# Reordering transposes and casts in a fused attention and feed-forward kernel

## The chip, the cores and the metric

The kernel runs on one core of one Trainium2 chip. The metric is the device time of one execution in microseconds (us), as the median of several runs. A profile of one execution gives the span of the core's instructions and the start and length of nearly all of them. Engines are called PE (TensorE), DVE (VectorE), ACT (ScalarE), POOL (GpSimd) and SP (SyncE, which only issues transfers here).

## The reference

Attention with 4 batches, 8 heads, 768 tokens and 64 columns a head. A query sees a key only if both fall to the same one of 16 centroids. Its output is the input of a gated feed-forward layer with 512 inputs and 1536 inner columns.

```
q_assign = argmax(q_n @ c_n.T); k_assign = argmax(k_n @ c_n.T)      # per head
scores   = where(q_assign == k_assign, q @ k.T / 8, -1e9)
x        = softmax(scores) @ v                                      # heads side by side: (3072, 512)
xn       = x / sqrt(mean(x*x) + 1e-6) * rms_g
out      = (silu(xn @ w_gate) * (xn @ w_val)) @ w_out
```

## The kernel before, in words

Work is cut into 8 units of 384 query tokens; a batch is two units. Heads are prepared in 8 groups of four, two groups to a batch. The order of everything is written out by hand: each engine runs its instructions in the order in which the Python code issues them, and waits on semaphores.

**Preparation of a head.** `trans(g, h, part)` turns q (part 0) or k (part 1) with three fp32 PE transposes into a PSUM tile `tq` (L208), which ACT or DVE copies to `qkT` (L214, L212). `cast` then copies `qkT` as bf16 into `qext` and `kext`, in two halves e = 0 and 1 (L227): q by POOL, k by DVE in the later groups. `vcast` casts v on POOL (L230). For a group, `cluster_products` (tile `sc`, L241) and DVE steps find each token's centroid as a one-hot row `oh`; `place` (L282) sends these rows by 8 small transfers for q and 8 for k into rows 64 to 79 of `qext` and `kext`, so that one product of 80 rows holds score and mask. Groups 0 and 1 use DVE transposes out of tables `pads` instead, whose unused columns POOL clears (L290, L571).

**Attention.** `scores(u, h, i)` makes two products into the PSUM tile `s` (two buffers, L332), and ACT takes the exponential into `pT` (L336); three such steps make a head of a unit. `pv` multiplies `pT` with v (`acc`, 18 products, L350), one head late: it is issued after the next head's second scores. The loop over a unit's 24 score steps is `attention`, which puts the other work between the steps: fixed hooks, or a list `fill` spread by its costs.

**Feed-forward.** In unit u the list holds the feed-forward of unit u - 1 and the output product of unit u - 2. `gv` makes `gate` and `val` (4 products of 384 columns each, L421). ACT takes the tanh of `gate` into `th` (L429), DVE multiplies it with `gate` again (L430), and a second DVE operation multiplies with `val` into `gvT` (L434). `out_mm` makes the output rows (`o`, L446).

**The shared PSUM buffers.** `tq`, `sc`, `gate`, `val`, `o` and the transposes of `xn` (`tx`) all take the next of three buffers of the pool `ps_g`, in the order of issue. So each of them waits until the one three places before it has been read for the last time: a `tq` by its copy, a `gate` by DVE's L430 (after ACT's L429), a `val` by DVE's L434.

**Where groups are prepared.** `group_work(g)` gives three lists: `t`, the 8 transposes in the order q, k of head 0, q, k of head 1 and so on; `c`, the casts (for each head one entry with POOL's q casts, `vcast`, the next loads and DVE's k cast of half 0, and one entry with DVE's k cast of half 1); and `a`, the centroid steps. `group(g)` orders them as two transposes and two cast entries of a head, then the next head. Groups 4 to 7 are spread with 16 of the `gate`/`val` entries in units 2 to 5. Group 3 is prepared in unit 1, in the list `prep`, after POOL's casts of group 2 (`norm`, which begins with a small POOL copy that waits for unit 0's normalised rows `xn`) and group 2's `vcast`, loads and centroid steps. `place` of group 2 is issued on SP, that of the others on POOL.

**Transfers.** SP's transfers cycle through eight semaphores in the built program, so each waits, besides its own data, for the landing of the transfer eight places before it. The weights are loaded from POOL's queue (`load_gv`, L194, and `load_o`, L197).

Of the kernel before, what the change touches and what calls it, by code (L numbers as in the profile page):

```python
# [22 lines left out]
def kernel(  # L23
# [12 lines left out]
    nc = tc.nc  # L36
    B, H, S, D = q.shape
    NC = centroids.shape[1]
# [6 lines left out]
    HG = 4  # L45
    NG = B * H // HG
    UNITS = [(b, c, HT) for b in range(B) for c in (0, HT)]
# [143 lines left out]
    def load_gv(i):  # L191
        c = slice(i * DF // 4, (i + 1) * DF // 4)
        for w, of in ((wg, moe_w_gate), (wv, moe_w_val)):
            nc.gpsimd.dma_start(out=w[:, :, c], in_=of[:, c].rearrange("(c p) f -> p c f", p=P))  # L194
# [34 lines left out]
    def vcast(n):  # L229
        nc.gpsimd.tensor_copy(vbf[n // HG % 4][:, n % HG, :, :D], stagedv[n])  # L230
# [46 lines left out]
    def place(on, g, m):  # L277

        ext = (kext if m else qext)[g % 4]
        for h in range(HG):  # L280
# [6 lines left out]

    pads = [(xp if p == 0 else outp).tile([P, NB, 32, 2], BF16, tag="o_sb" if p else "gvT", name=f"pads{p}")
            for p in range(H // 2)]
    nc.gpsimd.memset(pads[0][:, :, NC:], 0.0)  # L290

    def slot(n, m):

# [28 lines left out]
    def scores(u, h, i):  # L322
        b, col, nt = UNITS[u]
        g, hh, w = b * 2 + h // HG, h % HG, nt * P
        if i == 0:
            pT[u, h] = ptp.tile([P, ST, UQ], BF16, tag="pT", name="pT")
        n = ST // nt
        ps = ps_s.tile([P, 2, 512], F32, tag="s", name="s")
        flat = ps.rearrange("p a b -> p (a b)")
        for j in range(n):  # L330
            kc = n * i + j
            nc.tensor.matmul(ps[:, j, :w] if nt == HT else flat[:, j * w:(j + 1) * w],  # L332
                             lhsT=cols(kext[g % 4][:KR, hh], g, kc // HT, kc % HT * P, (kc % HT + 1) * P),
                             rhs=cols(qext[g % 4][:KR, hh], g, col // HT, 0, w), start=True, stop=True)
        of = ps[:, :, :w] if nt == HT else flat[:, :n * w].rearrange("p (c w) -> p c w", w=w)
        nc.scalar.activation(pT[u, h][:, n * i:n * i + n, :w], of, ACT.Exp, bias=off, scale=scale * ZS)  # L336
# [3 lines left out]
    def pv(u, h):  # L340
        b, _, nt = UNITS[u]
        g, hh = b * 2 + h // HG, h % HG
        if h == 0:
            xs[u] = xp.tile([P, HT, DM], F32, tag="x", name="x", bufs=2)
        if h % 2 == 0:
            accs[u] = ps_a.tile([P, 2, HT, D + 1], F32, tag="acc", name="acc")
        acc = accs[u]
        for t in range(nt):
            for kc in range(ST):
                nc.tensor.matmul(acc[:, h % 2, t], lhsT=pT[u, h][:, kc, t * P:(t + 1) * P],  # L350
                                 rhs=vbf[g % 4][:, hh, kc % HT * 2 + kc // HT], start=kc == 0, stop=kc == ST - 1)
        if h % 2:
            inv = small.tile([P, 2, HT], F32, tag="inv", name="inv")
            invs[u] = inv
            nc.vector.reciprocal(inv[:, :, :nt], acc[:, :, :nt, D])
            dst = xs[u][:, :nt, (h - 1) * D:(h + 1) * D].rearrange("p t (h d) -> p h t d", d=D)
            nc.vector.tensor_tensor(dst, acc[:, :, :nt, :D],  # L357
                                    inv[:, :, :nt].unsqueeze(3).broadcast_to([P, 2, nt, D]), op=ALU.mult)
# [6 lines left out]
    def squares(u, t, last):  # L365
        if (t, last) == (0, False):
            sq[u] = small.tile([P, 2, HT], F32, tag="ss", name="ss")
            xn[u] = xp.tile([P, HT, DM], BF16, tag="xn", name="xn")
        c = slice(DM - 2 * D, DM) if last else slice(0, DM - 2 * D)
        to = sq[u][:, int(last), t:t + 1]  # L370
        if u <= 1:
            nc.vector.scalar_tensor_tensor(xn[u][:, t, c], xs[u][:, t, c], 1.0 / DM, xs[u][:, t, c], op0=ALU.mult,
                                           op1=ALU.mult, accum_out=to)
        else:
            nc.scalar.activation(xn[u][:, t, c], xs[u][:, t, c], ACT.Square, scale=DM ** -0.5, accum_out=to)
# [90 lines left out]
    def group_work(g):  # L466

        t, c = [], []
        for h in range(HG):
            n = g * HG + h  # L470
            t += [(0.3, lambda h=h: trans(g, h, 0)), (0.3, lambda h=h: trans(g, h, 1))]

            def others(n=n):
                vcast(n)
                load_qk(n + NQ)
                load_v(n + NV)

            def both(h=h, f=others):
                cast(nc.gpsimd, g, h, 0)
                f()  # L480
                cast(nc.vector, g, h, 1, (0,))
            if g == 2:
                c.append((0.0, others))
            else:
                c += [(0.0, both), (0.0, lambda h=h: cast(nc.vector, g, h, 1, (1,)))]
        a = []
        for m in range(2):
            a += [(0.0 if i else 0.7, f) for i, f in enumerate(cluster_steps(g, m))]
            if g <= 3:
                a.append((0.0, lambda m=m: place(nc.sync if g == 2 else nc.gpsimd, g, m)))  # L490
        if g > 3:
            a.append((0.0, lambda: [place(nc.gpsimd, g, m) for m in range(2)]))
        return t, c, a

    def group(g):
        t, c, a = group_work(g)
        return [x for h in range(HG) for x in t[2 * h:2 * h + 2] + c[2 * h:2 * h + 2]] + a

    def spread(a, b):

# [10 lines left out]
    def ffn_work(u):  # L511
        n = UNITS[u][2] / HT
        w = [(0.18 * n, lambda c=c: xtrans(u, c)) for c in range(CC)]
        for f in range(FC):
            for val in (False, True):
                w.append((0.64 * n, lambda f=f, val=val: gv(u, f, val)))
        return w

    def out_work(u):
        return [(0.86, lambda t=t, p=p: out_mm(u, t, p)) for t in range(UNITS[u][2]) for p in range(3)]  # L520

    def border(o, ffn):

        return o[:-2] + ffn[:2] + o[-2:-1] + ffn[2:4] + o[-1:]
# [42 lines left out]
    casts(pool_, 0, Q1)  # L567
    casts(pool_, 1, Q1)
    vcast(0)
    for p in range(1, H // 2):  # L570
        nc.gpsimd.memset(pads[p][:, :, NC:], 0.0)  # L571
    load_gv(0)
    vcast(1)

# [53 lines left out]
    def attention(heads, fill, skip=0, hooks={}):  # L628
        gaps = [(u, h, i) for u, h in heads for i in range(UNITS[u][2])]
        total, done, n = sum(c for c, _ in fill), 0.0, 0  # L630
        for at, (u, h, i) in enumerate(gaps):
            scores(u, h, i)
            if i == min(1, UNITS[u][2] - 1):
                for p in due:
                    pv(*p)
                due[:] = [(u, h)]
            if h == H - 1:
                squares(u, i, False)
            if (u, h, i) in hooks:
                hooks[u, h, i]()  # L640
            while n < len(fill) and at >= skip and done <= total * (at + 1 - skip) / (len(gaps) - skip):
                done += fill[n][0]
                fill[n][1]()
                n += 1
        for _, f in fill[n:]:
            f()

    attention([(0, h) for h in range(H)], [], hooks={(0, *divmod(i, HT)): f for i in range(H * HT) for f in [first.get(i, more)] if f})
    for u in range(1, NU):
        ffn, o, g = ffn_work(u - 1), out_work(u - 2) if u > 1 else [], u + 2  # L650
        if u == 1:
            t, c, a = group_work(2)
            t3, c3, a3 = group_work(3)
            n = LEAD - 4
            prep = c + a + [x for h in range(HG) for x in t3[max(2 * h, n):2 * h + 2] + c3[2 * h:2 * h + 2]] + a3[:5]
            idle = const.tile([P, 1], BF16)

            def norm():
                rms(0)
                nc.gpsimd.tensor_copy(idle, xn[0][:, HT - 1, DM - 1:])  # L660
                for h in range(HG):
                    casts(pool_, H + h, K0, Q0, K1, Q1)
                    if h:
                        load_o((h - 1) * FC // 3)

            hooks = {(1, 0, 0): late[6], (1, 0, 1): lambda: (late[7](), norm())}
            hooks.update({(1, *divmod(2 + i, HT)): t3[i][1] for i in range(n)})
            hooks[1, *divmod(LEAD - 1, HT)] = lambda: (busy(4, False), xtrans_all(0))
            fill = spread(ffn[CC:CUT], prep)
            attention([(1, h) for h in range(H)], fill, LEAD, hooks)  # L670
        else:
            fill = ffn_work(u - 2)[CUT:] + [(0.0, lambda u=u: rms(u - 1))]
            fill += border(spread(o[:3], a3[5:]) + o[3:], ffn) if u == 2 else border(o, ffn)
            attention([(u, h) for h in range(H)], fill + spread(ffn[CC:CUT], group(g) if g < NG else []), 1)
# [41 lines left out]
```

The softmax here doesn't subtract the row's maximum and nothing guards it: scores larger than these inputs give would overflow.

## Time and profile before

| what | value |
|---|---|
| median of 8 runs | 349.37 us (348.44 to 349.99) |
| the profiled execution: time, span | 349.42 us, 347.6 us |
| PE busy | 338.5 us (97%) |
| ACT, DVE, POOL busy | 260.0 us (75%), 221.6 us (64%), 111.8 us (32%) |
| chain of work that ended last | PE 83%, ACT 6%, POOL 6%, DVE 3% of the span |

Busy time is that of the engine's instructions. An entry such as "PE ... [0.84 <-DVE th L430]" in the timeline says that PE sat idle for 0.84 us before this instruction, and that the DVE instruction on line 430 ended the wait. Each timeline row is start, length, engine, line, operation, output<-inputs, shape and how many were merged. A row for several matmuls begins with the first and ends with the last one's modelled end, which overlaps the next row's start.

### The profile page before, as it was taken

To read this page: it belongs to the slowest core of one execution; us is meant where nothing else is said; L and a number is where in the kernel's file an instruction comes from. 1 tells how busy PE (TensorE), PEld (TensorE's weight loads), DVE (VectorE), ACT (ScalarE), POOL (GpSimd) and SP (SyncE) were. 2 spreads that over 40 slices of the span, in tenths; PEclk is the share of its full clock that TensorE was granted. 3 is DMA by queue.
4 is the path that set the end of the run, shared out by engine and by line. 5 is a ranking of instruction groups with operands and counts; after the bars stand their busy time and mean duration, and the time that the engine had idled before them with its cause. 6 is when DMAs were issued, how large, how long until landed. Compare 5 with 4: busy or idle time off the path is not lost.

```text
span 347.6 us, 7983 instructions
## 1 busy us (share of the span) xinstructions
PE 338.5 (97%) x3039; PEld 208.0 (60%) x3039; DVE 221.6 (64%) x539; ACT 260.0 (75%) x449; POOL 111.8 (32%) x225
## 2 busy tenths in 40 slices
PE   8999999999999999999999999999999999999996
PEld 4547656555665557655675657755566656655553
DVE  6999686966568645786267854687456644675430
ACT  5899978766888769887787877978778877764321
POOL 5999595234344403371041801436000000000000
PEclk9999999999999999999999999999999999999999
DMA  7999999073350015401130001000100001001002
GB/s 277 395 180 256 251 176 284 28 235 123 107 183 29 16 60 159 147 17 40 60 93 2 23 33 62 0 6 19 62 32 0 2 33 60 2 1 63 30 2 91
DMA packets 27158, 31.62 MB, mean 91 GB/s; under 512 B 4464, under 2 KB 24176, under 8 KB 27120
## 3 DMA queue, kind: packets, MB, share of 16 engines
q1 hardware_dynamic: 18464, 25.02, 21.1%
q0 software_dynamic: 8368, 5.71, 10.2%
q8 instruction: 24, 0.39, 0.4%
q10 hardware_dynamic: 288, 0.39, 0.3%
q14 instruction: 14, 0.11, 0.1%
HBM read 28.35 MB, written 6.29 MB: 100 GB/s over the span
## 4 chain that ended last, share of the span: by engine, by line
PE 83%; ACT 6%; POOL 6%; DVE 3%; issue 1%; POOLq 0%; ACTq 0%; DVEq 0%
PE o L446 17%; PE val L421 17%; PE gate L421 17%; PE s L332 15%; PE acc L350 8%; ACT pT L336 4%; PE tq L208 3%; PE sc L241 3%; POOL kext L227 2%; POOL qext L227 2%; PE tx L395 1%; PE warm L117 1%; PE o L457 1%; DVE th L430 1%; POOL vbf L230 1%
## 5 line engine op out<-in xcount | busy, mean ns | idle before, releaser
L336 ACT ACTIVATE pT<-s,off 128x768 bf16<-128x768 f32 x192 | 170.8, 905 | 36.0 <-PE s L332 35.2
L332 PE MATMUL s<-qext,kext 80*128 80x384 bf16 x384 | 94.4, 327 | 2.6 <-ACT pT L336 0.8
L421 PE MATMUL gate<-xnT,wg 128*128 128x384 bf16 x384 | 78.4, 325 | 0.6 <-DVE gvT L434 0.4
L421 PE MATMUL val<-xnT,wv 128*128 128x384 bf16 x384 | 78.1, 326 | 0.8 <-DVE th L430 0.8
L430 DVE SCALAR_TENSOR_TENSOR th<-th,gate 128x384 f32<-128x384 f32 x84 | 46.4, 552 | 50.6 <-ACT th L429 50.5
L446 PE MATMUL o<-wo,gvT 128*128 128x512 bf16 x276 | 67.4, 379 | 0.0
L227 POOL CAST qext<-qkT 64x384 bf16<-64x384 f32 x64 | 34.4, 543 | 78.2 <-ACT qkT L214 54.4
L332 PEld LDWEIGHTS <-kext 80*128 80x128 bf16 x384 | 36.4, 98 | 33.3 <-issue 8.7
L421 PEld LDWEIGHTS <-wv 128*128 128x128 bf16 x384 | 36.1, 97 | 26.3 <-issue 4.6
L429 ACT ACTIVATE th<-gate 128x384 f32<-128x384 f32 x84 | 41.1, 490 | 14.3 <-PE gate L421 13.9
L434 DVE SCALAR_TENSOR_TENSOR gvT<-th,val 128x384 bf16<-128x384 f32 x84 | 46.2, 550 | 8.8 <-PE val L421 4.2
L421 PEld LDWEIGHTS <-wg 128*128 128x128 bf16 x384 | 35.7, 97 | 25.2 <-issue 3.9
L350 PEld LDWEIGHTS <-pT 128*128 128x128 bf16 x1152 | 43.4, 97 | 8.9 <-DVE x L357 0.4
L350 PE MATMUL acc<-vbf,pT 128*128 128x65 bf16 x1152 | 45.5, 193 | 0.0
L446 PEld LDWEIGHTS <-gvT 128*128 128x128 bf16 x276 | 25.8, 97 | 25.1
L208 PE MATMUL tq<-ident_f,qk 128*128 128x128 f32 x192 | 29.8, 275 | 0.4 <-DVE scT L307 0.4
L214 ACT ACTIVATE qkT<-tq 128x384 f32<-128x384 f32 x57 | 26.6, 497 | 3.5 <-PE tq L208 3.2
L396 DVE TENSOR_SCALAR xnT<-tx,gcol 128x384 bf16<-128x384 bf16 x28 | 10.6, 413 | 28.7 <-PE tx L395 28.7
L282 POOL DMA_DIRECT2D qext<-oh x40 | 19.1, 486 | 29.6 <-DVE oh L271 29.6
L208 PEld LDWEIGHTS tq<-ident_f,qk 128*128 128x128 f32 x192 | 23.3, 141 | 7.1 <-issue 0.8
L449 ACT COPY o_sb<-o 128x512 f32<-128x512 f32 x23 | 13.5, 586 | 17.4 <-PE o L446 17.4
L282 POOL DMA_DIRECT2D kext<-oh x40 | 19.1, 484 | 10.7 <-DVE oh L271 10.7
(82 smaller groups left out, 249.8 us busy)
## 6 DMA issues: line engine op xcount, KB each, us to landing
qk<-in_q_dram SPq DMA_DIRECT2D x32, 192.0 KB, 3.9
vs<-in_v_dram SPq DMA_DIRECT2D x32, 192.0 KB, 4.0
out_dram<-o_sb SPq DMA_DIRECT2D x23, 256.0 KB, 2.0
qk<-in_k_dram SPq DMA_DIRECT2D x30, 192.0 KB, 3.9
wg<-in_moe_w_gate_dram POOLq DMA_DIRECT2D x4, 384.0 KB, 8.0
wv<-in_moe_w_val_dram POOLq DMA_DIRECT2D x4, 384.0 KB, 10.1
wo<-in_moe_w_out_dram POOLq DMA_DIRECT2D x3, 512.0 KB, 7.2
qext<-oh POOLq DMA_DIRECT2D x40, 12.0 KB, 1.6
```

The costliest lines, as they stand in the source:

```text
L208: nc.tensor.transpose(ps[:, i * P:(i + 1) * P], qk[:, part, 2 * i:2 * i + 2].rearrange("p t d -> p (t d)"), ident_f)
L214: nc.scalar.activation(to, ps, ACT.Copy, scale=by)
L227: on.tensor_copy(to, of)
L282: on.dma_start(out=ext[D:D + NC, h, e * UQ:(e + 1) * UQ], in_=put[g, m][32 * h + e * NC:32 * h + (e + 1) * NC])
L332: nc.tensor.matmul(ps[:, j, :w] if nt == HT else flat[:, j * w:(j + 1) * w], lhsT=cols(kext[g % 4][:KR, hh], g, kc // HT, kc % HT * P, (kc ...
L336: nc.scalar.activation(pT[u, h][:, n * i:n * i + n, :w], of, ACT.Exp, bias=off, scale=scale * ZS)
L350: nc.tensor.matmul(acc[:, h % 2, t], lhsT=pT[u, h][:, kc, t * P:(t + 1) * P], rhs=vbf[g % 4][:, hh, kc % HT * 2 + kc // HT], start=kc == 0 ...
L421: nc.tensor.matmul(ps, lhsT=w[:, c, f * P:(f + 1) * P], rhs=xnT[u][:, c, :n], start=c == 0, stop=c == CC - 1)
L429: nc.scalar.activation(th, ps, ACT.Tanh, scale=0.5)
L430: nc.vector.scalar_tensor_tensor(th, th, 1.0, ps, op0=ALU.add, op1=ALU.mult)
L434: nc.vector.scalar_tensor_tensor(gvT[u][:, f, :n], gates[u], 0.5, ps, op0=ALU.mult, op1=ALU.mult)
L446: nc.tensor.matmul(outs[u], lhsT=gvT[u][:, f, t * P:(t + 1) * P], rhs=wo[:, f], start=f == 0, stop=f == FC - 1)
```

## The change

Three edits. The tables `pads` are all cleared on POOL before the first cast, where before three of the four were cleared after the first `vcast`. The transposes and casts of a group are no longer issued head by head: after the first two transposes, one transpose of the next head and one cast entry take turns. The same is done for group 3 in unit 1. And the product with v of unit 0's last head is issued after unit 1's first scores, not after its second.

```diff
     pads = [(xp if p == 0 else outp).tile([P, NB, 32, 2], BF16, tag="o_sb" if p else "gvT", name=f"pads{p}")
             for p in range(H // 2)]
-    nc.gpsimd.memset(pads[0][:, :, NC:], 0.0)
+    for of in pads:
+        nc.gpsimd.memset(of[:, :, NC:], 0.0)
...
+    def weave(t, c):
+
+        return [x for pair in zip(t, c) for x in pair] + c[len(t):]
+
     def group(g):
         t, c, a = group_work(g)
-        return [x for h in range(HG) for x in t[2 * h:2 * h + 2] + c[2 * h:2 * h + 2]] + a
+        return t[:2] + weave(t[2:], c) + a
...
     vcast(0)
-    for p in range(1, H // 2):
-        nc.gpsimd.memset(pads[p][:, :, NC:], 0.0)
     load_gv(0)
...
             scores(u, h, i)
-            if i == min(1, UNITS[u][2] - 1):
+            if i == (0 if (u, h) == (1, 0) else 1):
                 for p in due:
                     pv(*p)
...
             n = LEAD - 4
-            prep = c + a + [x for h in range(HG) for x in t3[max(2 * h, n):2 * h + 2] + c3[2 * h:2 * h + 2]] + a3[:5]
+            prep = c + a + weave(t3[n:], c3) + a3[:5]
```

No instruction is added or removed on any engine. On SP the order stays as it was; on POOL only the three clears move. The order in which PE meets the pieces in units 3, 4 and 5 (one letter names one `gate`/`val` pair; counted from the built programs):

```
before: gate_a tq1 s acc val_a tq2 gate_b s val_b tq3 s tq4 gate_c val_c s acc tq5 gate_d s tq6 val_d s gate_e tq7 tq8 s acc val_e gate_f
after:  gate_a tq1 s acc val_a tq2 tq3 s gate_b val_b s tq4 gate_c tq5 s acc val_c tq6 s gate_d val_d s tq7 gate_e tq8 s acc val_e gate_f
```

## The prediction

> **What bounds the kernel now.** I read the page's busy shares first, then the table of stretches for the units that prepare groups, then the timeline around every place where PE waits. From the page, and from the stretches (columns: us, PE, PE weight loads, DVE, ACT, POOL busy, granted clock, DMA share, GB/s):
>
> ```profile
> PE 338.5 (97%) x3039; PEld 208.0 (60%) x3039; DVE 221.6 (64%) x539; ACT 260.0 (75%) x449; POOL 111.8 (32%) x225
> ```
> ```profile
> 122.00:163.00 41.00, 41.00 (x381) 25.66 (x378) 26.14 (x65) 32.74 (x61) 13.66 (x28) 1.00 0.26 83
> 163.00:204.00 41.00, 41.00 (x381) 25.66 (x378) 26.11 (x65) 32.74 (x60) 13.67 (x28) 1.00 0.14 45
> 204.00:245.00 41.00, 41.00 (x388) 25.80 (x384) 26.70 (x66) 33.08 (x60) 13.67 (x28) 1.00 0.07 26
> ```
>
> Units 3, 4 and 5, where groups 5 to 7 are prepared, keep PE busy without a gap. A reorder can't win anything there; any wait that it makes is added to the end. PE does wait in units 1 and 2. Timeline, unit 1, then unit 2:
>
> ```profile
> 53.32 0.82 PE L208 MATMUL tq<-ident_f,qk 128*128 128x128 f32 x6
> 53.46 0.88 DVE L227 CAST kext<-qkT 64x384 bf16<-64x384 f32 x2
> 54.37 0.56 DVE L430 SCALAR_TENSOR_TENSOR th<-th,gate 128x384 f32<-128x384 f32 x1
> 54.98 0.81 PE L421 MATMUL val<-xnT,wv 128*128 128x384 bf16 x4 [0.84 <-DVE th L430]
> ```
> ```profile
> 91.21 0.49 PE L332 MATMUL s<-qext,kext 80*128 80x384 bf16 x2
> 91.54 0.82 PE L421 MATMUL gate<-xnT,wg 128*128 128x384 bf16 x4
> 91.80 0.90 ACT L336 ACTIVATE pT<-s,off 128x768 bf16<-128x768 f32 x1
> 92.19 0.81 PE L421 MATMUL val<-xnT,wv 128*128 128x384 bf16 x4
> 92.58 0.49 ACT L429 ACTIVATE th<-gate 128x384 f32<-128x384 f32 x1
> 93.10 0.56 DVE L430 SCALAR_TENSOR_TENSOR th<-th,gate 128x384 f32<-128x384 f32 x1 [0.60 <-ACT th L429]
> 93.17 1.09 PE L208 MATMUL tq<-ident_f,qk 128*128 128x128 f32 x6
> 93.69 0.36 DVE L227 CAST kext<-qkT 64x384 bf16<-64x384 f32 x1
> 94.08 0.56 DVE L434 SCALAR_TENSOR_TENSOR gvT<-th,val 128x384 bf16<-128x384 f32 x1
> 94.69 0.81 PE L421 MATMUL gate<-xnT,wg 128*128 128x384 bf16 x4 [0.43 <-DVE gvT L434]
> ```
>
> Both are the pool of three PSUM buffers. At 54 the `val` is third after a `gate`; two k casts ran first on DVE. At 93 the second of two adjacent `tq` waits for the `gate` of 91.54, and the next `gate` for the `val` of 92.19. This second excerpt is the ruler for all that follows. Unhindered, the fourth `tq` would start after `gate`, `val`, `s` and one `tq`: 0.65 + 0.65 + 0.33 + 0.33 = 1.96 us after 91.54, at 93.50 (these are the distances between starts where PE runs without a gap). Its first record is at 93.72, 0.06 after L430's end at 93.66. So **a gate's buffer is free 2.18 us after its start**: 0.82 on PE, 0.22 until ACT has finished the `pT` ahead, 0.52 to DVE's start, 0.62 to the release. **A val's buffer is free about 1.0 us after that L430 has ended**, with one k cast and L434 between (94.69 against 93.66).
>
> At the end of unit 1 a third wait stands, and its releaser is not named:
>
> ```profile
> 65.37 4.97 SPq L282 DMA_DIRECT2D kext<-oh  x8
> 67.20 0.98 PE L332 MATMUL s<-qext,kext 80*128 80x384 bf16 x4 [0.79 <-issue]
> ```
>
> These are unit 2's first scores; they need group 2's one-hot k rows. The transfer issued at 65.37 landed at 67.11, the second (issued at 65.95) at 67.72; PE started at 67.20, and its fourth product at 67.86. PE arrived there at 66.25.
>
> **What the Trainium skill says.** "Perfetto Trace Analysis", Optimization Strategy: a gap that repeats on the engine that should be saturated can mean that there is not enough PSUM for the next tile. The trace agrees: the 0.84 and the 0.22 + 0.59 us at 54 and 93 are such gaps. "TensorE: Matmul & The Clock Gate", on engine queue depths: ACT and DVE are strictly first in, first out. It agrees: at 54 L430 starts only when two casts (0.88 us) are through. "SBUF — State Buffer", two separate sides: DVE operations with two SBUF inputs and GpSimd operations that read SBUF lock each other out of a shared port. It agrees: L372 takes 0.92 us at 32.74 beside POOL casts, 0.52 at 66.02 without.
>
> **Clears ahead of the casts.** Three POOL clears (1.13 us at 14.83 to 15.96) move into POOL's idle 3.11 us before 5.08, where the first clear takes 0.42; they fit, and if they slow DVE's small operations of 2 to 3 us at all, it is by 0.1. POOL then is 1.07 us earlier until about 36, the four weight loads with it. POOL was the releaser of one PE wait in there (0.49 us before 25.97) and through it of ACT's 0.37 us before 26.57, from where ACT runs without a gap until 34.70. So ACT gains about 0.4 us there. DVE is busy without a gap through this stretch and sets `xn` at 39.68; it gains little (0 to 0.3, as port conflicts move).
>
> **pv(0, 7) one step earlier.** It needs the last `pT` of head 7: ACT's three of 32.21 end one by one 0.8 apart, that one at 33.9. So PE, which did a `tq` at 33.51, would sit from 33.50 to 33.95, do `acc` (0.55), and start that `tq` at 34.50. ACT wants its result at 34.59 and gets it near 35.0: 0.4 us lost on ACT. For that DVE's `inv` (35.05) could start at 34.97 only, as L212 of 34.42 is ahead of it: 0.08 won. With the clears: about nothing.
>
> **Unit 1's group 3.** Now `gate tq s ...` take turns and one k cast stands before L430. Step by step with durations 0.65, 0.33 (`s`, `tq`), 0.55 (`acc`): a `gate` or `val` meets its buffer's next user 2.84 us later, above 2.18, so the wait at 54 goes, and 0.12 at 61.8: 1.1 us. But PE then reaches unit 2's scores at about 65.1 and waits 2 us instead of 0.95. The k rows' arrival depends on none of this: SP works through its list, each transfer behind the landing of the eighth before. The v load issued at 50.54 landed only at 57.57, behind weight loads[...]; the k load issued at 57.59 had waited for just that. Then come one v load, 8 q rows at about 0.63 us each, the k rows. So the 1.1 us is **worth nothing at the end**, and the same gate swallows whatever the first 40 us win or lose. What can move it is the weights' DMA backlog starting 1.07 us earlier; DMA was 0.98 to 1.03 busy from 28 to 36, so I take 0.3 us earlier (0 to 0.6; at worst 0.2 later).
>
> **Units 3, 4, 5.** Counting three places back in the new order: `gate_c` needs `gate_b`'s buffer, `tq5` that of `val_b`; again `gate_e` and `tq8` with `gate_d` and `val_d`. Between starts of `gate_b` and `gate_c` lie `gate`, `val`, `s`, `tq`: 0.65 + 0.65 + 0.33 + 0.33 = 1.96 us, exactly the ruler's distance, also with an `s` just ahead whose `pT` makes ACT late. Freed at 2.18 to 2.25 (if a `tq` copy also delays that `pT`): **0.22 to 0.29 us of wait.** `tq5` follows at 0.65 more, 2.83 to 2.90; `val_b` is freed at 2.90 to 3.15 (L430's start to `gvT`'s end took 1.28 us at 137.23 and 1.54 at 93.10, plus 0.06; in the new order a k cast stands between again): 0.07 to 0.32. Together 0.29 to 0.61, I take 0.45, twice a unit: 0.9. What goes is 0.09 (`tq` 135.28 to `gate` 135.69 is 0.41 for 0.33). Net 0.8 a unit, **2.4 us for three** (1.5 to 3.4). Behind a waiting `gate` stand the next scores on PE, and behind those ACT's `pT`; ACT is busy for 32.7 of 41 us and catches up, so nothing is added. Nor is anything given back: PE has no gap until 245, and after it waits only for work that it released itself.
>
> **Unit 2's group 4.** Same new order but for the first `tq5`, which has an `s` and `acc` ahead: 0.25 + 0.45 = 0.7 new for 0.81 old: -0.1.
>
> **Sum.** -0.3 - 0.1 + 2.4 = +2.0 us. The profiled execution took 349.42 us, 0.05 above the median: 351.4.
>
> **Rivals.** (1) *The group's waits go and none come* (faster). For it: each k cast now stands alone before L430, and the two waits at 54 and 93 were 1.65 us. It needs ACT to take the `th` at once; at 92.58 it was 0.22 late, so against. If freed within 1.96, and if the k rows come a whole POOL step (1.07) earlier, then -1.0 - 0.8 - 0.3 = 347.3. It decides at 1.96 us of release. (2) *Small waits and an earlier gate cancel*: lower ends, 1.5 - 0.6 - 0.1 = +0.8, or less still if DVE overlaps its casts as at 137: 349.4 to 350.1. (3) *The gate comes later*: earlier weight loads push SP's loads, k rows 0.5 us late, and upper ends of the waits: +0.5 + 3.0 = 352.9. (4) The edit doing nothing is excluded: the built programs differ in order on PE, ACT and DVE.
>
> **Numbers.** A measurement of this kernel tells about 0.2% (0.7 us) from no change. Main case (350.2 to 352.6) 0.66; rival 1 0.17; rival 2 0.13; rival 3 0.04. Slower 0.70, same 0.13, faster 0.17. Range 348.4 to 352.8.
>
> **What would show it.** Right: in units 3 to 5 PE waits of 0.2 to 0.3 on a `gate` released by DVE L430, then 0.1 to 0.3 on a `tq` released by DVE L434, twice a unit; PE busy below 41.0 in 41; no wait near 54; about 2 us of unnamed wait before unit 2's first scores, still near 67. Wrong: units 3 to 5 without gaps, or the scores of unit 2 starting a microsecond earlier.

## The result, and the profile after

The changed kernel takes **351.81 us** (median of 11 runs, 351.07 to 352.85) against 349.42 us (median of 32) for the kernel before on the same chip: ratio 1.007, 95% interval 1.0059 to 1.0082. It is slower by 2.4 us. Its profiled execution took 351.07 us with a span of 349.3 us; the one of before took 349.42 with 347.6. Line numbers of the changed kernel are one higher than before from `scores` on (L430 is now L431, L434 is L435).

The busy line of the page says little: PE is busy for 98% of a longer span.

```profile
PE 340.9 (98%) x3039; PEld 208.1 (60%) x3039; DVE 220.4 (63%) x539; ACT 259.8 (74%) x449; POOL 113.0 (32%) x225
```

The stretches say where. Same columns as before (us, PE, PE weight loads, DVE, ACT, POOL, clock, DMA share, GB/s); the cuts are 42 us apart now, since a unit takes 41.9 us in place of 41.04:

```profile
122.00:164.00 42.00, 41.67 (x378) 25.62 (x377) 26.24 (x65) 32.68 (x59) 13.67 (x28) 1.00 0.25 82
164.00:206.00 42.00, 41.67 (x379) 25.56 (x377) 26.25 (x65) 32.68 (x59) 13.66 (x28) 1.00 0.13 44
206.00:248.00 42.00, 41.67 (x378) 25.64 (x377) 26.81 (x67) 32.97 (x60) 13.67 (x28) 1.00 0.07 23
```

PE was busy in 41.00 of 41.00 us in these units; now it stands still for 0.33 us in each, and more is hidden in ends that are modelled. The timeline of unit 3 shows the first pair of waits:

```profile
134.25 0.55 DVE L431 SCALAR_TENSOR_TENSOR th<-th,gate 128x384 f32<-128x384 f32 x1 [1.72 <-ACT th L430]
134.26 0.49 PE L208 MATMUL tq<-ident_f,qk 128*128 128x128 f32 x3
...
134.72 0.35 DVE L227 CAST kext<-qkT 64x384 bf16<-64x384 f32 x1
...
134.86 0.81 PE L422 MATMUL gate<-xnT,wg 128*128 128x384 bf16 x4
...
134.99 0.54 DVE L435 SCALAR_TENSOR_TENSOR gvT<-th,val 128x384 bf16<-128x384 f32 x1
...
135.58 0.31 PEld L208 LDWEIGHTS tq<-ident_f,qk 128*128 128x128 f32 x3 [0.30 <-DVE gvT L435]
135.59 0.55 PE L208 MATMUL tq<-ident_f,qk 128*128 128x128 f32 x3
```

The reader is to compare starts. The `tq` of 134.26 is three products 0.11 apart, so the `gate` could start at 134.59. It starts at 134.86, 0.06 after L431's end at 134.80: 0.27 us of wait. L431 had itself waited for ACT's `th`. The next `tq` could start 0.65 later, at 135.51; it starts at 135.59, 0.06 after `gvT`'s end, because a k cast (134.72) and L435 came in between: 0.08. The buffer that the `gate` of 134.86 takes is that of the `gate` started at 132.63, 2.23 us before.

The second pair of the unit stands at 140.33 and 141.31 and waits 0.22 and 0.33; here the buffers are those of the `gate` of 138.16 and of the `val` behind it:

```profile
138.16 0.81 PE L422 MATMUL gate<-xnT,wg 128*128 128x384 bf16 x4
138.81 0.81 PE L422 MATMUL val<-xnT,wv 128*128 128x384 bf16 x4
...
139.72 0.56 DVE L431 SCALAR_TENSOR_TENSOR th<-th,gate 128x384 f32<-128x384 f32 x1 [1.09 <-ACT th L430]
...
140.33 0.81 PE L422 MATMUL gate<-xnT,wg 128*128 128x384 bf16 x4
...
140.70 0.56 DVE L435 SCALAR_TENSOR_TENSOR gvT<-th,val 128x384 bf16<-128x384 f32 x1
...
141.31 0.55 PE L208 MATMUL tq<-ident_f,qk 128*128 128x128 f32 x3 [0.17 <-DVE gvT L435]
```

The same four waits stand in units 4 and 5, equal to 0.01 us. The table of waits names only the `tq` half of them, and only in part (us in total, times, longest):

```profile
PE tq L208 <- DVE gvT L435: 0.7, 4, 0.2
```

In unit 1 the wait of 0.84 us on L430 is gone; `val` follows `tq` without a gap:

```profile
53.41 0.81 PE L422 MATMUL gate<-xnT,wg 128*128 128x384 bf16 x4
...
54.40 0.50 PE L208 MATMUL tq<-ident_f,qk 128*128 128x128 f32 x3
...
54.74 0.81 PE L422 MATMUL val<-xnT,wv 128*128 128x384 bf16 x4
```

And unit 2's first scores start at 66.15 in place of 67.20, with SP's transfers of the k rows issued from 63.84 in place of 65.37 (the first two landed at 66.06 and 66.67, before at 67.11 and 67.72):

```profile
63.84 4.18 SPq L282 DMA_DIRECT2D kext<-oh  x6
...
65.30 0.81 PE L422 MATMUL val<-xnT,wv 128*128 128x384 bf16 x4
...
66.15 0.98 PE L333 MATMUL s<-qext,kext 80*128 80x384 bf16 x4
```

PE was through with the `val` at 65.95, so it waited 0.20 us for these rows, where the kernel before waited 0.95.

The difference of the two profiled executions, read at the first scores of each unit, goes: -1.05 us at unit 2, -1.02 at unit 3, then +0.90, +0.88 and +0.90 over units 3, 4 and 5, and no more to the end: +1.66, as the spans say (349.3 - 347.6).

The medians differ by 2.39, not by 1.66: the profiled execution of the changed kernel took 0.74 us less than its median. With +0.03 from unit 2 and +2.68 from units 3 to 5, the medians leave about -0.3 for all that lies ahead of unit 2. The interval of the ratio is 0.4 us wide either way, so this -0.3 can't be told from nothing. What varies between executions lies there: units 3 to 5 take the same 41.93 us each in the other profile that has this order (below), and from unit 6 on the profiles of all the kernels agree to 0.02 us.

### The profile page after: what moved, and what is told of

Its sections match the earlier page's. It is cut to its first block, busy times and chain, and to the rows that moved or that the text cites. A ratio compares the mean times of both kernels' runs of the same rounds, so it can differ in the third digit from the quotient of the medians.

```text
span 349.3 us, 7982 instructions
## 1 busy us (share of the span) xinstructions
PE 340.9 (98%) x3039; PEld 208.1 (60%) x3039; DVE 220.4 (63%) x539; ACT 259.8 (74%) x449; POOL 113.0 (32%) x225
## 4 chain that ended last, share of the span: by engine, by line
PE 81%; ACT 12%; DVE 4%; issue 1%; POOL 0%; ACTq 0%; DVEq 0%; POOLq 0%
PE o L447 17%; PE val L422 16%; PE gate L422 15%; PE s L333 15%; PE acc L351 9%; ACT pT L337 7%; PE tq L208 3%; ACT qkT L214 3%; PE sc L241 3%; DVE th L431 1%; PE tx L396 1%; ACT th L430 1%; PE warm L117 1%; DVE gvT L435 1%; PE o L458 1%
## 5 line engine op out<-in xcount | busy, mean ns | idle before, releaser
L431 DVE SCALAR_TENSOR_TENSOR th<-th,gate 128x384 f32<-128x384 f32 x84 | 46.3, 552 | 52.3 <-ACT th L430 52.1
L227 POOL CAST qext<-qkT 64x384 bf16<-64x384 f32 x64 | 35.4, 560 | 75.9 <-ACT qkT L214 71.1
L435 DVE SCALAR_TENSOR_TENSOR gvT<-th,val 128x384 bf16<-128x384 f32 x84 | 46.2, 550 | 9.2 <-PE val L422 4.4
L430 ACT ACTIVATE th<-gate 128x384 f32<-128x384 f32 x84 | 41.2, 491 | 14.0 <-PE gate L422 13.9
L208 PE MATMUL tq<-ident_f,qk 128*128 128x128 f32 x192 | 31.3, 281 | 1.0 <-DVE gvT L435 0.7
```

The lines of the kernel that those rows point to most:

```text
L208: nc.tensor.transpose(ps[:, i * P:(i + 1) * P], qk[:, part, 2 * i:2 * i + 2].rearrange("p t d -> p (t d)"), ident_f)
L227: on.tensor_copy(to, of)
L430: nc.scalar.activation(th, ps, ACT.Tanh, scale=0.5)
L431: nc.vector.scalar_tensor_tensor(th, th, 1.0, ps, op0=ALU.add, op1=ALU.mult)
L435: nc.vector.scalar_tensor_tensor(gvT[u][:, f, :n], gates[u], 0.5, ps, op0=ALU.mult, op1=ALU.mult)
```

## The experiments

Each was timed beside the kernel before on its chip (medians 349.23, 349.31 and 349.04 us in the three groups of runs); a ratio is to that kernel, from all runs and not from the two medians, so the two can differ a little where runs scatter.

### The order of groups 4 to 7, taken out and put in alone

The changed kernel with the old order of `group`:

```
-        return t[:2] + weave(t[2:], c) + a
+        return [x for h in range(HG) for x in t[2 * h:2 * h + 2] + c[2 * h:2 * h + 2]] + a
```

> The changed kernel with groups 4 to 7 in the old order (two transposes, two casts of a head); unit 1's group 3, the clears and pv(0, 7) stay changed. Theory (the order of groups 4 to 7 alone makes the loss, by waits for the three PSUM buffers): PE has no wait of 0.2 to 0.3 us on DVE L431 in units 3 to 5, these units take 0.8 to 0.9 us less each, and the time is 351.8 - 2.7 = 349.1 us or a little less (348.4 to 349.5). Rival (the earlier pv(0, 7), or unit 1's order, costs part of it): 350 us or more.

Measured: 348.76 us, ratio 0.9988 (0.9980 to 0.9996). Units 3 to 5 take 41.03 to 41.05 us each again, and unit 2's old waits of 0.22 and 0.59 are back.

The kernel before with only that edit, the other way round:

> The kernel before with only groups 4 to 7 in the new order. Theory: +0.9 us in each of units 3, 4 and 5, nothing in unit 2 (new waits for old ones), nothing before it: 349.4 + 2.7 = 352.1 us (351.5 to 352.6). Rival (the loss needs the other edits too): below 351 us.

Measured: 351.97 us, ratio 1.0079 (1.0067 to 1.0091): 2.74 us more. Units 3 to 5 take 41.93 us each. So the whole loss, 2.7 us, is the new order in `group`, and the rest of the change is worth 0.5 us the other way (0.1 to 0.7).

### The alternation of group 3 alone

```
-            prep = c + a + [x for h in range(HG) for x in t3[max(2 * h, n):2 * h + 2] + c3[2 * h:2 * h + 2]] + a3[:5]
+            prep = c + a + weave(t3[n:], c3) + a3[:5]
```

> The kernel before with only unit 1's group 3 in the new order. Theory (the 1.1 us that it wins at 54 us is waited off again at unit 2's first scores, which stand still until group 2's k rows land): the wait at 54 is gone, PE waits about 2 us before unit 2's first scores, which start at 66.5 to 67.3 us as before, and the time is 349.4 us within 0.4. Rival (the k rows follow PE): first scores at about 66.1, 348.3 us.

Measured: 349.29 us, ratio 1.0004 (0.9985 to 1.0023), with a wide scatter (347.93 to 351.72). The wait at 54 was gone; in the profiled execution PE came to unit 2's first scores at about 65.1 and waited 0.92 us and 0.17 more. So 1.1 us of PE wait was removed, and in the median nothing came out at the end. This agrees with a wait for the k rows behind it (a gate, as it is called from here on), but the interval would not tell 0.5 us of gain from none. The profiled execution is no support for the theory: PE waited 1.1 us and not about 2, the scores started at 66.14 and it took 348.36 us, which is what the rival named. It lies 0.9 below its own median. The rows did not follow PE, which stood waiting for them; they landed at 66.05 for 67.11, and what made them earlier is not shown.

### Clears alone, and the products with v alone

Two kernels, each the kernel before with one of the two small edits.

> The kernel before with only the clears of the tables moved ahead of the first casts. Theory: unit 1's first scores 0.2 to 0.4 us earlier than 33.17, swallowed by the wait for group 2's k rows: the time of the kernel before within 0.3 us, unit 2's first scores at 66.8 to 67.3. Rival: the weight loads that POOL issues 1 us earlier bring the k rows, and with them unit 2 and the end, 1 us earlier: 348.3.

Measured: 349.25 us, ratio 0.9995 (0.9986 to 1.0004). No difference that can be told, as expected. Counted from the first scores of all, unit 1's came 0.20 us earlier than before. Unit 2's start at 66.37, below the band named and 0.83 earlier than before, but in an execution of 348.58 us, 0.7 below its own median; so that isn't evidence for the rival.

> The kernel before with only unit 0's last products with v ahead of unit 1's second scores. Theory: 0.4 us more at unit 1's third scores (50 and on), swallowed by the wait for group 2's k rows: the time of the kernel before within 0.3 us. Rival: the loss goes through to the end: 0.4 us more.

Measured: 349.72 us, ratio 1.0011 (1.0003 to 1.0019): 0.4 us slower, as much as was lost at once: from unit 1's first scores to those of its head 1 it took 3.18 us for 2.76. (What the expectation calls the third scores are the second.) The median goes with the rival. The profile doesn't show a way for it. A possible way is that POOL copies one column of unit 0's `xn` before it casts group 2, and issues the three loads of `wo` among those casts, so that a later `xn` would mean later `wo` loads, and later landings of the loads and k rows that SP issues behind them:

```profile
40.23 0.19 POOL L660 COPY idle<-xn 128x1 bf16<-128x1 bf16 x1 [3.28 <-DVE xn L385]
...
50.01 0.74 POOL L197 DMA_DIRECT2D wo<-in_moe_w_out_dram  x1
```

In the kernel before the copy was at 39.82, the third load at 49.22 and the landing of the first k rows at 67.11; here the rows landed at 67.57. But this execution's first scores began at 10.60 for 10.10. Counted from there, the copy came 0.1 us earlier, the third load 0.3 later and the k rows at 56.97 for 57.01, so no later; PE's wait for them was 0.52 for 0.95. In this execution, then, the gate took the loss up, and what is later is its start. What made the 0.4 us of the median stays open; a run further below, which takes the edit back in another kernel, can't settle it.

Singly, the three small edits come to about +0.3 us (clears -0.2, group 3 +0.1, products with v +0.4, by their ratios), while together, in the changed kernel with the old order, their ratio makes -0.4. The uncertainty of the sum is some 0.8 us, so this isn't a contradiction, but which of the three brings the gain isn't known.

### The k casts off DVE

The changed kernel, with the k casts of groups 4 to 7 on POOL:

```
-                cast(nc.vector, g, h, 1, (0,))
+                cast(nc.gpsimd if g > 3 else nc.vector, g, h, 1, (0,))
```

and the same for the other half.

> The changed kernel with the k casts of groups 4 to 7 on POOL in place of DVE; nothing else. Theory (the first wait of each pair is set by ACT and L431, the second by the k cast that stands between L431 and L435): the gates in units 3 to 5 still wait 0.22 to 0.27 us, the tq waits of 0.08 and 0.33 go, in unit 2 the 0.33 goes: 3 x 0.41 + 0.33 = 1.6 us less, 350.2 us (349.8 to 350.6). Rival A, the k cast is also what holds L431: all waits go, 348.9 or less. Rival B, the tq waits come from the chain gate, val itself: 351.8 as before, no gain. A POOL cast takes 0.51 us where DVE took 0.35; POOL was busy for a third of these units, so it is not expected to be late.

Measured: 350.14 us, ratio 1.0025 (1.0015 to 1.0036). Against the changed kernel's ratio of 1.007 that is 1.6 us less, as expected. The timeline of the same place:

```profile
134.34 0.56 DVE L431 SCALAR_TENSOR_TENSOR th<-th,gate 128x384 f32<-128x384 f32 x1 [1.72 <-ACT th L430]
...
134.95 0.81 PE L422 MATMUL gate<-xnT,wg 128*128 128x384 bf16 x4
...
135.00 0.55 DVE L435 SCALAR_TENSOR_TENSOR gvT<-th,val 128x384 bf16<-128x384 f32 x1
...
135.61 0.55 PE L208 MATMUL tq<-ident_f,qk 128*128 128x128 f32 x3
```

L435 starts 0.66 after L431 and not 0.74, so the `tq` starts 0.66 after the `gate`: no wait. The `gate` still comes 0.05 after L431's end, 0.27 late; at 140.36 it is 0.22 late, and the `tq` of 141.02 is on time. A unit takes 41.55 us: 0.38 less, for 0.41 worked out. The two waits of a pair have separate causes: ACT's chain to L431 for the first, the k cast ahead of L435 for the second.

### The same alternation, one place earlier

```
-        return t[:2] + weave(t[2:], c) + a
+        return t[:1] + weave(t[1:], c) + a
```

> The changed kernel with the alternation of groups 4 to 7 begun one place earlier (t0, t1, c0, t2, c1, ... in place of t0, t1, t2, c0, t3, c1, ...): the same instructions, still one cast between two transposes. Counted three places back, no gate's buffer is now wanted sooner than 2.29 us after its start in units 3 to 5 (1.96 before); in unit 2 one is still wanted after 1.96. Theory (what decides is the distance to the third buffer back against a release of 2.2 us): the gate waits of units 3 to 5 go, and with them the tq waits behind them: 2.7 us less, and perhaps 0.3 in unit 2: 349.0 us (348.6 to 349.7). Rival (alternating itself costs, one cast ahead of each L431 or L435): 351 or more.

Measured: 347.69 us, ratio 0.9963 (0.9946 to 0.9981), with runs from 347.38 to 349.55. It is faster than both kernels, and the median is 1.3 us better than expected. The stretches of units 3 to 5:

```profile
122.00:163.00 41.00, 41.00 (x377) 25.75 (x376) 26.19 (x66) 32.79 (x60) 13.77 (x28) 1.00 0.27 84
163.00:204.00 41.00, 41.00 (x378) 25.80 (x377) 26.19 (x65) 32.82 (x60) 13.77 (x28) 1.00 0.14 45
204.00:245.00 41.00, 41.00 (x378) 25.82 (x377) 26.69 (x65) 33.40 (x60) 13.76 (x28) 1.00 0.06 19
```

PE stands still nowhere; a unit takes 40.96 us, 0.08 less than before, since the old wait of 0.09 is gone too. The same casts alternate with the same transposes: **the distance to the third buffer back decides, not the alternation**. In units 3 to 5 every `gate` was read for the last time at least 0.14 us before its buffer's next user came: where that distance is shortest, 2.28 us, the reading ended 1.93 to 2.14 us after the start.

Where the extra gain came from: all of unit 2's 0.81 us went (42.01 us for 42.83), where one wait of 0.25 had been expected to stay. At that place, a `tq` 1.97 us after a `gate`, the recorded wait is on ACT's semaphore and not on DVE's, and the product starts at 92.82, before that gate's L431 has ended at 92.98, so it had been given another buffer; it starts 0.05 after ACT has copied the `tq` before it.

Buffers are therefore not always handed out in turn. In the kernel before the same shows once in each of units 3 to 5: the `gate` of 135.69 starts 0.05 after ACT's copy of the `tq` of 134.62 has ended (135.64), and 0.20 before L434 has read the `val` three places back (135.90). In the changed kernel no `tq`, `sc`, `gate` or `val` of units 2 to 5 starts before its third buffer back is read, so the prediction's count holds there.

The same kernel with the products with v put back behind unit 1's second scores:

> The changed kernel with the alternation begun one place earlier (as in the run that shifts it by one) and unit 0's last products with v back behind unit 1's second scores. Theory after the run of that edit alone (0.4 us more at the end, with POOL's third wo load 0.3 us later after the start of the first scores, and the k rows with it): 347.3 us, unit 2's first scores near 66.1. Rival, as predicted (the wait for the k rows swallows it): 347.7, as with the edit.

Measured: 347.76 us, ratio 0.9962 (0.9949 to 0.9975), against 0.9963 with the edit: no difference that can be told, though with intervals of 0.5 and 0.6 us either way 0.4 us could hide. Its profiled execution (347.09 us) had the scores of unit 1's head 1 at 35.72 for 36.73 (0.57 of it from an earlier start of the first scores of all), reached unit 2's first scores at 65.0 and waited 0.94 us there, for 0.53 with the edit. In these two profiles the gate did swallow it.

### What stands at the gate

The kernel before with group 3's alternation, and group 2's one-hot rows sent head by head:

```
-                a.append((0.0, lambda m=m: place(nc.sync if g == 2 else nc.gpsimd, g, m)))
+            a.append((0.0, lambda: [place(nc.sync, g, m, [h]) for h in range(HG) for m in range(2)]))
```

> The same as the kernel before with only unit 1's group 3 in the new order, but group 2's one-hot rows are sent head by head (q and k of head 0 first), not all of q and then all of k. Theory (the k rows' place on SP's queue is the gate): head 0's k rows land near 63 us, PE has no wait before unit 2's first scores, and the 1.1 us of unit 1 and the 0.95 us of waiting both go: 349.4 - 2.1 = 347.3 us (346.9 to 347.8). Rival (something else ends that wait, such as the fetch of instructions or the loads of v): no gain over the run with unit 1's order alone.

Measured: 348.50 us, ratio 0.9984 (0.9975 to 0.9993). The wait at unit 2's first scores was gone, but a third of the expected 2.1 us came out. Another wait stands in front, for head 15's q:

```profile
58.29 0.52 PE L208 MATMUL tq<-ident_f,qk 128*128 128x128 f32 x3 [0.28 <-DMA qk<-in_q_dram]
```

It came 0.45 us late, and 0.2 to 0.3 us each were lost at 66.50 (ACT's `pT`) and 69.93 (L430). Both the rows and this load are issued after the `wo` loads. So the third `wo` load was moved, in the shifted kernel without the v edit:

```
-                    if h:
+                    if 0 < h < 3:
...
-            prep = c + a + weave(t3[n:], c3) + a3[:5]
+            prep = c + a + weave(t3[n:], c3) + [(0.0, lambda: load_o(2 * FC // 3))] + a3[:5]
```

> That kernel with the third of the three wo loads moved on POOL from about 49.5 us to behind the casts of group 3, about 62.5 us. Theory (SP's loads of q, k and v issued from 50.8 us land behind wo's bytes, and SP's row transfers stand behind their landings): those loads land 3 to 4 us earlier, the first k rows before 64 us, the wait ahead of unit 2's first scores (0.5 + 0.2 us in the kernel shifted by one) goes, PE reaches them at about 65.9: 0.6 us less than without the move, 346.7 us (346.4 to 347.2). Rival (the landings are slow for another reason, or the row transfers wait for DVE): k rows as late as before and no gain, or, if wo's third part comes late for unit 2's o products at 75 to 78 us, a loss.

Measured: 347.75 us, ratio 0.9970 (0.9953 to 0.9986), scattered from 346.78 to 351.15. The profiled execution is one of the long ones (350.78 us), and shows why. Timeline, then stretches:

```profile
61.26 0.74 POOL L197 DMA_DIRECT2D wo<-in_moe_w_out_dram  x1
...
62.39 5.50 SPq L282 DMA_DIRECT2D kext<-oh  x8
...
68.14 0.85 PE L333 MATMUL s<-qext,kext 80*128 80x384 bf16 x4 [2.50 <-issue]
```
```profile
68.10:70.20 2.10, 2.06 (x24) 1.66 (x25) 0.18 (x1) 1.48 (x2) 1.84 (x4) 0.66 0.46 131
70.20:72.30 2.10, 2.10 (x9) 0.99 (x8) 1.05 (x3) 0.70 (x2) 2.02 (x5) 0.53 0.80 229
```

SP's loads did land earlier than in the shifted kernel without the move, though by 0.6 to 1.5 us and not by the 3 to 4 expected (head 15's q at 56.81 for 57.39, the last of them at 60.62 for 61.65). In this execution the second `wo` load, which was not moved, landed only at 56.98 for 53.59 there; why is not known. But the moved load was issued 1.1 us ahead of the k rows; these landed from 68.05, after the load itself (67.19), and PE waited 2.7 us. The first of them took 5.7 us from issue to landing, for 1.7 in the kernel before. PE's granted clock then fell: it is 0.66 and 0.53 in the two stretches, and `gate` products stand 0.32 apart for 0.16. Other executions took 346.8 to 347.2, which fits the rows getting through first; no profile shows one of these. What is shown is that in this execution the k rows issued just behind a `wo` load landed late: the move had put the load at a worse place.

With both, so that the first heads' k rows are ahead of that load:

> The kernel with the later wo load, and group 2's one-hot rows sent head by head (q, q, k, k of head 0 first). If the later load has removed the wait for the k rows: no further gain, within 0.3 us of it. If the wait stands still: it goes here, 0.6 us less.

Measured: **346.87 us**, ratio 0.9936 (0.9924 to 0.9948), with all five runs in 346.54 to 347.02. This is the fastest kernel of the study, 2.2 us below the kernel before.

```profile
57.47 1.17 SPq L282 DMA_DIRECT2D kext<-oh  x2
...
61.02 0.74 POOL L197 DMA_DIRECT2D wo<-in_moe_w_out_dram  x1
...
65.23 0.98 PE L333 MATMUL s<-qext,kext 80*128 80x384 bf16 x4
```

The first k rows are issued at 57.47, ahead of the load, and landed at 60.09; unit 2's scores start at 65.23 without waiting for them. SP's loads of q, k and v landed 1.7 to 2.4 us earlier than in the shifted kernel without either edit. The scatter is gone with the wait, as far as five runs can tell, which supports the reading that the gate is what varies between executions. The rows head by head without the later load were not run in the shifted kernel, so how much of the 0.9 us below that kernel each of the two brings isn't known.

## Why the prediction was right

The time was 351.81 for 351.4, and the loss came where and how it was named: in units 3 to 5, by buffers wanted sooner than they are released. Ahead of unit 2 the account is weaker. By its steps:

- **Units 3, 4, 5: right.** The ruler held: buffers of the `gate`s came free 2.23 and 2.17 us after their starts (132.63 to 134.86, 138.16 to 140.33), for 2.18 to 2.25; those of the `val`s 2.96 and 3.15 us after the same starts, for 2.90 to 3.15. So the two pairs fell on the two ends of the range, 0.35 and 0.55 with a mean of the 0.45 taken. A unit lost 0.9 and not 0.8: a `tq` that has waited starts its second product 0.055 us later than others, twice a unit, which the step had left out. 2.68 us for 2.4. The run with k casts on POOL and the one with the shift showed the two causes separately.
- **Unit 2: mechanism right, size off by 0.1.** 0.27, 0.22 and 0.33 came for the old 0.22 and 0.59: +0.03 for -0.1.
- **Unit 1: right.** The wait at 54 went, and group 3's alternation alone brought nothing measurable.
- **The gate: its sign failed in the profiled execution.** The prediction named unit 2's scores "still near 67", behind about 2 us of wait, and called a start a microsecond earlier a sign of being wrong. They started at 66.15 for 67.20, behind 0.20 us of wait. PE came at 65.95 and not at 65.1: this execution's first scores were 0.55 later, the clears and the v edit together cost 0.21, and unit 1 gave 1.06. And the k rows landed 1.05 earlier. Why is not shown: in the ten profiles that send these rows in the same order and leave the `wo` loads in place, they landed anywhere from 65.83 to 67.57. One execution was not enough to read a step that varies so much.
- **The gate in the median: not shown.** -0.3 had been taken (0 to 0.6), and the medians leave -0.3, but with 0.4 us of uncertainty either way. That the total came so near owes something to luck here.
- **"The k rows' arrival depends on none of this": not settled.** Where the `wo` load stands does move the k rows, as the last two runs show. The products with v, moved alone, cost 0.4 us in the median and nothing at the gate of their profile; in the shifted kernel no cost could be told. How much of the first 40 us passes the gate stays open.
- **Clears: size off.** Unit 1's first scores came 0.23 us earlier relative to the first of all, for 0.4 on ACT; the v edit cost 0.44 there for 0.4. Together about a loss of 0.2 and not nothing, too small to see at the end.
- **Rivals.** The first (waits go, none come) named 1.96 us of release as its point of decision, and release was 2.2. The shifted kernel shows what it would have been: 347.69 us, near the 347.3 worked out. Of its gain of 1.6 us in the median, the waits of units 2 to 5 make 1.0, where the rival counted 1.1; the rest lies ahead of unit 2. In the third rival the upper ends of the waits, by the prediction's own figures, come to 3.4 us and not 3.0, so its sum should have been 353.3.

## What to carry over

With k buffers handed out in turn, or nearly so, write down for each user how long its buffer is held from start to release, taken from a place where PE is seen to wait, and compare it with the distance in issue time to the k-th user behind; a reorder that makes the average distance more even can still push one pair under it, and one place of shift can put it right. A saturated engine gives no wait back: four waits of 0.1 to 0.3 us a unit, hardly seen in the table of waits, were the whole result. Before taking a wait away ahead of a transfer, find what the transfer itself stands behind; here a weight load that is first used some 20 us after it has landed was part of it, and with that load moved and the rows sent head by head the wait was gone.

## What the runs showed of the hardware

In the profile of the kernel with the later `wo` load alone, PE waited 2.7 us, ran its next four products 0.16 us apart, and then, from about 68.8 to 72.2, went at half clock: 3.4 us. The Trainium skill, "TensorE: Matmul & The Clock Gate", in its part on the clock gate, puts the fall to half rate after at least one idle window of about 3.4 us; here a wait of 2.7 us was enough, and the measurement decides.

The first scores of an execution started at 10.09 to 10.83 us in the profiles of this study, with the same instructions ahead of them on PE. In the profile of before the first fp32 transposes stood 0.11 us apart from 3.93 us on; in that of after 0.21 apart until about 5.7. The same part says that the first 3.4 us of work run at half rate and that its end varies between runs; the trace agrees in kind, though the clock column shows 1.00 there. Between these two profiles the first scores lie 0.55 us apart; how much of that is still there at the end of an execution was not measured.
